# Order edges for the casts of formed right operands and for one sum of blocks, in a fused attention and expert kernel

## The chip, the cores and the metric

The program runs on one core of one Trainium2 chip. The metric is the device time of one execution in microseconds; times are medians over runs. The core's engines are TensorE (PE, with its weight loads as PEld), VectorE (DVE), ScalarE (ACT), GpSimd (POOL) and SyncE (SP), which issues nearly all DMAs here.

## The reference

Two attentions follow each other, and a weighted sum of four experts follows them. Each of 8 batches has 8 heads, 576 tokens and a head width of 64; 32 learned rows `p` are packed against `k` and `v`, and the tokens `q` then attend to those packed rows.

```python
def sm_attn(qq, kk, vv):
    s = scale * np.matmul(qq, kk.transpose(0, 1, 3, 2))
    a = np.exp(s - np.max(s, axis=-1, keepdims=True))
    return np.matmul(a / (np.sum(a, axis=-1, keepdims=True) + 1e-09), vv)
p_packed = sm_attn(p, k, v)
x = sm_attn(q, p_packed, p_packed)          # then (8 * 576, 512)
pr = domain_probs / (domain_probs.sum(-1, keepdims=True) + 1e-09)
out = sum(pr[:, e:e+1] * (np.maximum(x @ w1[e], 0) @ w2[e]) for e in range(4))
```

## The kernel before

**Units.** The 8 batches are taken in four pairs (`sb`), and the 4 experts' 1024 hidden columns in 8 chunks of 512 (`ch`). A unit is one batch and one chunk; the list `units` has 64 of them, pair by pair and chunk by chunk, the even batch ahead of the odd one (two neighbours are swapped at the start and two at the end). Below, "unit 21" is `u == 21`.

**The second product of a unit.** The product of the hidden block with `w2` is done as seven smaller products instead of eight (`ORDER`: a11, s3, s1, s2, a22, s4, a12). A left operand is either a block `a..` of the hidden activations, left by VectorE in the tile `ablk`, or a sum or difference of blocks, made by VectorE at line 598 in the tile `sblk`: s3 = a11 - a21, s1 = a21 + a22, s2 = s1 - a11, s4 = a12 - s2. Each left operand is split into a high part, which ScalarE casts (line 111, tile `st`), and a low part, which GpSimd subtracts (line 115, `st`). The order of these casts among themselves, and of the low parts among themselves, is fixed by edges from each to the one before (`marks["operand"]`). They are issued two products ahead (`LA = 2`), so the first operands of unit u + 1 are issued beside the last products of unit u.

**The right operands.** They are formed from `w2` once, while the first pair of batches is worked on (`t_form`), kept in `tt` tiles, and stored to DRAM (`td`) for later pairs. For chunk ch + 1 this is done in the odd units of the first pair from unit 3 on and in the even unit behind each: loads of b11, b12, b2, then seven steps. t1 and t3 are made ahead of step 1, t2 ahead of step 3 and t4 ahead of step 4; t1, t2 and t4 all replace the contents of b11, which step 0 casts, so t1 waits until step 0 has read it. t1 and t4 are GpSimd's, t2 and t3 VectorE's (line 639). Each step casts the high part on ScalarE (line 111, `tt<-b` or `tt<-ablk`) and subtracts the low part on GpSimd (line 115).

**Attention beside it.** `pack_unit` works on the packed rows of the next pair of batches in units 4 and 7 (first pair of batches), 17 and 20, 33 and 36, with scores at product 4 or, in units 20 and 36, at product 5. Its steps are: scores on TensorE; the maximum over keys on VectorE (line 182); the bias (184 or 186); the exponential on ScalarE (188); a transposition of the result on TensorE (line 75); a copy to SBUF (111, `at`); the product with `v`; its scaling (`ppn`, line 221 on ScalarE or 223 on VectorE); another transposition. With `relief=True`, which is the case in units 4 to 8, ScalarE first copies the scores to SBUF (line 180), and takes the bias and the scaling. `tok_unit` does the second attention in the same manner.

**First product.** `g_form` multiplies the packed rows into `w1` (tile `wraw`), ScalarE casts the result (`ghl`, 111) and VectorE leaves the low part (`ghl`, 115); `mm1_groups` multiplies it with the tokens `xh`, `xl`, and VectorE evicts the block at line 370. VectorE adds the products of the second matmul up at line 718.

**Who sets the order.** The kernel is built with a planner that works through the program in a simulated time and writes one list for each engine. On the chip each engine goes through its list in order, and semaphores stop it where data is not there. `after(ins, prev)` adds an edge that only tells the planner to put `ins` behind `prev`. TensorE's work may move between calls of `together`. PSUM holds four tiles (`dbl`) in turn, so TensorE can be about three groups of matmuls ahead of VectorE's and ScalarE's reads.

Of the kernel before, what the change touches and what calls it, by code (L numbers as in the profile page):

```python
# [42 lines left out]
def attention_moe(ctx: ExitStack, tc: tile.TileContext, q, k, v, p, dp, w1, w2, out):  # L43
# [107 lines left out]
    def pack_unit(bs, g, new, relief=False):  # L151
        nfull = S // P
        r = S - nfull * P
        kts = {}
        for b in bs:
            if g == 0:
                pts[b] = small.tile([P, NPAIR, NPK], F32, name="pt")
                nc.sync.dma_start(out=pts[b], in_=p[b])
            kts[b] = new(b, [P, 2, S], "kt")
            nc.sync.dma_start(out=kts[b], in_=k[b][:, 2 * g:2 * g + 2, :])  # L160
        yield

        def load_v(b):
            vt, vr = new(b, [P, nfull, 4 * D], "vt"), new(b, [P, 4 * D], "vr")
            behind_w1(nc.sync.dma_start(
                out=vt, in_=v[b, 0:nfull * P, g * 4 * D:(g + 1) * 4 * D].rearrange("(c p) d -> p c d", p=P),
            ), b)
            behind_w1(nc.sync.dma_start(out=vr[0:r], in_=v[b, nfull * P:S, g * 4 * D:(g + 1) * 4 * D]), b)
            return [vt[:, c, :] for c in range(nfull)] + [vr]

        vt = load_v(bs[0])
        yield
        pss = scores(bs, g, lambda b, pr, hh: pts[b][hh * D:(hh + 1) * D, pr, :], kts)
        a1s, rss = {}, {}
        for b in bs:
            nb = small.tile([P, 1], F32, name="nb")
            a1s[b] = new(b, [P, S], "a1")
            a1v, raw = a1s[b].rearrange("p (c s) -> p c s", c=2), pss[b][:, :, 0:HS]
            if relief:
                nc.scalar.copy(out=a1v, in_=raw)  # L180
                raw = a1v
            nc.vector.tensor_reduce(out=nb, in_=raw, axis=AX.XY, op=ALU.max)
            if relief:
                nc.scalar.mul(nb, nb, -SCALE)
            else:
                marks["bias", b, g] = nc.vector.tensor_scalar_mul(nb, nb, -SCALE).ins
            sm = small.tile([P, 1], F32, name="sm")
            marks["first", b, g] = nc.scalar.activation(
                out=a1v, in_=raw, func=AF.Exp, scale=SCALE, bias=nb, accum_out=sm
            ).ins  # L190
            rss[b] = small.tile([P, 1], F32, name="rs")
            if relief:
                nc.scalar.activation(out=rss[b], in_=sm, func=AF.Copy, bias=1e-9)
            else:
                nc.vector.tensor_scalar_add(rss[b], sm, 1e-9)
            nc.vector.reciprocal(out=rss[b], in_=rss[b])
        yield
        prs = slice(2 * g, 2 * g + 2)
        for b in bs:
            if b != bs[0]:  # L200
                vt = load_v(b)
            at = new(b, [P, len(SC), P], "at")
            ps = dbl()
            for c in range(nfull):
                tr(out=ps[:, 0, c * P:(c + 1) * P], in_=a1s[b][:, c * P:(c + 1) * P], identity=ident)
            tr(out=ps[0:r, 1, 0:P], in_=a1s[b][:, nfull * P:S], identity=ident)
            turn = nc.vector if (b, g) == (0, 0) else nc.scalar
            hi_of(at[:, 0:nfull, :], ps[:, 0].rearrange("p (c s) -> p c s", s=P), turn)
            marks["turned", b, g] = hi_of(at[0:r, nfull, :], ps[0:r, 1, 0:P], turn).ins
            yield  # L210
            ps = dbl()
            for c, (_, n) in enumerate(SC):
                for h in range(4):
                    p0 = h // 2 * 2 * NPK + cols(b, h % 2).start
                    mm(
                        out=ps[p0:p0 + NPK, 0, 0:D], lhsT=at[0:n, c, p0:p0 + NPK],
                        rhs=vt[c][0:n, h * D:(h + 1) * D], start=c == 0, stop=c == len(SC) - 1,
                    )
            ppn = small.tile([P, D], F32, name="ppn")
            if relief:  # L220
                nc.scalar.mul(ppn, ps[:, 0, 0:D], rss[b])
            else:
                nc.vector.tensor_scalar_mul(ppn, ps[:, 0, 0:D], rss[b])
            yield
            ps = dbl()
            tr(out=ps[0:D, 0, 0:P], in_=ppn, identity=ident)
            psv = ps[0:D, 0, 0:P].rearrange("p (j n) -> p j n", j=2)
            for hh in range(2):
                hi_of(
                    ppbd[b % 4][hh * D:(hh + 1) * D, prs, cols(b, hh)], psv[:, :, cols(b, hh)],  # L230
                    nc.scalar if relief else nc.vector,
                )
            yield
# [354 lines left out]
    def s_operand(u, i):  # L588

        name = ORDER[i] if u < LAST else PLAIN[i]  # L590
        blk = lambda n: blocks[u, n]
        if name[0] == "s":
            t = hpool.tile([P, 2, HS], F32, name="sblk", bufs=3)
            x, y, op = {
                "s1": ("a21", "a22", ALU.add), "s2": ("s1", "a11", ALU.subtract),
                "s3": ("a11", "a21", ALU.subtract), "s4": ("a12", "s2", ALU.subtract),
            }[name]
            marks["sum", u, name] = nc.vector.tensor_tensor(out=t, in0=blk(x), in1=blk(y), op=op).ins  # L598
            blocks[u, name] = t
        src = blk(name)  # L600
        st = st_tile(F32R)
        parts = hi_of(both(st, 0), src, nc.scalar).ins, lo_of(both(st, 1), src, both(st, 0), nc.gpsimd).ins
        for ins, prev in zip(parts, marks.get("operand", ())):
            after(ins, prev)
        marks["operand"] = parts
        blocks[u, "op", i] = st
# [13 lines left out]
    def t_form(ch, new, eng):  # L620
# [14 lines left out]
        for i, name in enumerate(ORDER):  # L635
            n = of[name]
            for m in {"t3": ("t1", "t3"), "t2": ("t2",), "t4": ("t4",)}.get(n, ()):
                x, y, place = how[m]
                op = eng[m].tensor_tensor(out=blk[place], in0=blk[x], in1=blk[y], op=ALU.subtract).ins
                if ch == 1 and m == "t3":  # L640
                    after(op, marks["bias", 1, 1])
                blk[m] = blk[place]
            t = wpool.tile([P, 2, 2, DH], F32R, name="tt", bufs=8)
            high = hi_of(t[:, 0], blk[n], nc.scalar)
            lo_of(t[:, 1], blk[n], t[:, 0], nc.gpsimd)
            if ch == 1 and i == 0:
                after(high.ins, marks["operand"][0])
            if ch == 1 and i in (1, 3):
                after(high.ins, marks["turned", 1, i // 2])
            marks["form"] = high  # L650
            tt[ch, i] = t
            yield
# [329 lines left out]
```

## Time and profile before

| what | value |
|---|---|
| time, median of 3 runs (lowest to highest) | 1279.35 us (1279.25 to 1279.41) |
| the profiled execution: its own time, its span | 1280.87 us, 1279.1 us |
| mean granted TensorE clock | 0.997 |
| PE, PEld busy share of the span | 98%, 92% |
| DVE, ACT, POOL busy share of the span | 75%, 38%, 67% |

The span is the time from the first to the last instruction of the profiled execution; 1.77 us of that execution's own time lie around it. The median of the runs is 1.52 us below the profiled execution's time. A row of the timeline gives the start and length of one instruction, or of several alike in a row that are drawn together (x2: two), and in brackets the idle time of that engine just before it and what ended it.

### The profile page before, as it was taken

The numbers are of one execution on the slowest core, as the hardware profiler recorded it, in microseconds if no ns is written. First come the engines' busy times: TensorE is split into PE (matmuls) and PEld (weight loads), VectorE is DVE, ScalarE is ACT, GpSimd is POOL, SyncE is SP. The second block draws the span as 40 slices with busy tenths as digits, with TensorE's granted clock in tenths as the row PEclk, the third lists the DMA queues.
The fourth block names the chain that finished last, engine by engine and source line by source line (L and its number), as shares of the span: only waits on it lengthen the run. The fifth ranks groups of instructions, "written<-read, shape, count | busy, mean of one in ns | idle before, by whom it ended". The sixth has DMA issues, their size and how long they took to land.

```text
span 1279.1 us, 26863 instructions
## 1 busy us (share of the span) xinstructions
PE 1256.6 (98%) x10764; PEld 1171.7 (92%) x10764; DVE 955.1 (75%) x1299; ACT 492.4 (38%) x888; POOL 861.2 (67%) x570
## 2 busy tenths in 40 slices
PE   6999999999999999999999999999999999999998
PEld 4789988998999999999999999999999999999998
DVE  4776777899985767997786667799679567766776
ACT  3644444636334333333324423333323533332321
POOL 3878888898995555666578454576568755556575
PEclk9999999999999999999999999999999999999999
DMA  9885656534465544545455546433446443444562
GB/s 334 337 303 186 227 172 225 185 138 169 161 221 197 172 159 128 183 163 158 133 151 172 181 145 205 144 126 125 157 126 214 148 136 116 128 155 127 178 217 100
DMA packets 91707, 223.93 MB, mean 175 GB/s; under 512 B 9280, under 2 KB 32192, under 8 KB 91584
## 3 DMA queue, kind: packets, MB, share of 16 engines
q1 hardware_dynamic: 90768, 221.92, 52.4%
q8 instruction: 86, 1.41, 0.4%
q10 hardware_dynamic: 816, 0.30, 0.1%
q14 instruction: 37, 0.30, 0.1%
HBM read 183.31 MB, written 38.87 MB: 174 GB/s over the span
## 4 chain that ended last, share of the span: by engine, by line
PE 73%; POOL 11%; DVE 10%; issue 3%; ACT 2%; DMA 2%; SPq 0%; ACTq 0%; POOLq 0%; DVEq 0%
PE dbl L70 66%; POOL st L115 7%; PE dbl L80 6%; DVE sblk L598 2%; POOL acc L749 2%; DVE acc L718 2%; DVE ablk L370 1%; DVE ghl L115 1%; POOL tt L115 1%; DMA kt<-in_k 1%; PE dbl L75 1%; POOL xl L115 1%; ACT ghl L111 1%; DVE a L257 0%; DVE s L277 0%
## 5 line engine op out<-in xcount | busy, mean ns | idle before, releaser
L70 PE MATMUL dbl<-st,tt 128*128 128x288 f32 x5388 | 766.6, 296 | 4.4 <-DVE ghl L115 1.8
L70 PEld LDWEIGHTS dbl<-st,tt 128*128 128x128 f32 x5388 | 724.7, 188 | 49.1 <-issue 28.9
L115 POOL TENSOR_TENSOR st<-sblk,st 128x576 fp32r<-128x576 f32 x252 | 397.1, 1584 | 230.5 <-ACT st L111 221.8
L70 PE MATMUL dbl<-xh,ghl 128*128 128x288 f32 x2016 | 406.4, 294 | 2.1 <-DVE ghl L115 2.1
L115 POOL TENSOR_TENSOR st<-ablk,st 128x576 fp32r<-128x576 f32 x193 | 293.5, 1524 | 137.4 <-ACT st L111 131.0
L718 DVE TENSOR_TENSOR acc<-dbl,acc 128x576 f32<-128x576 f32 x385 | 287.7, 751 | 103.3 <-PE dbl L70 101.3
L70 PEld LDWEIGHTS dbl<-xh,ghl 128*128 128x128 f32 x2016 | 321.8, 188 | 2.7 <-DVE ghl L115 2.6
L70 PE MATMUL dbl<-xl,ghl 128*128 128x288 f32 x1008 | 295.8, 294 | 0.2 <-POOL xl L115 0.2
L370 DVE SCALAR_TENSOR_TENSOR ablk<-dbl,pbt 128x576 f32<-128x576 f32 x256 | 192.3, 752 | 138.7 <-PE dbl L70 137.0
L111 ACT CAST st<-sblk 128x576 fp32r<-128x576 f32 x252 | 170.3, 676 | 275.9 <-DVE sblk L598 220.4
L111 ACT CAST st<-ablk 128x576 fp32r<-128x576 f32 x193 | 130.3, 675 | 253.6 <-PE dbl L70 230.1
L70 PEld LDWEIGHTS dbl<-xl,ghl 128*128 128x128 f32 x1008 | 188.9, 188 | 0.5 <-POOL xl L115 0.5
L598 DVE TENSOR_TENSOR sblk<-ablk 128x576 f32<-128x576 f32 x126 | 134.4, 1067 | 9.6 <-DVE ablk L370 0.5
L111 ACT CAST ghl<-dbl 128x512 fp32r<-128x512 f32 x128 | 72.7, 588 | 114.1 <-DVE ghl L115 58.4
L115 DVE TENSOR_TENSOR ghl<-dbl,ghl 128x512 fp32r<-128x512 f32 x124 | 83.3, 687 | 20.5 <-ACT ghl L111 18.5
L598 DVE TENSOR_TENSOR sblk<-ablk,sblk 128x576 f32<-128x576 f32 x63 | 78.3, 1242 | 5.3
L80 PE MATMUL dbl<-wraw,ppbd 64*32 64x512 f32 x1024 | 68.2, 597 | 0.0
L115 POOL TENSOR_TENSOR tt<-b,tt 128x512 fp32r<-128x512 f32 x42 | 62.8, 1505 | 2.1 <-ACT tt L111 2.0
L598 DVE TENSOR_TENSOR sblk<-sblk,ablk 128x576 f32<-128x576 f32 x63 | 57.7, 916 | 1.3
L749 POOL TENSOR_TENSOR acc<-acc,acc 128x576 f32<-128x576 f32 x28 | 43.5, 1563 | 12.6 <-DVE acc L718 12.5
L716 ACT COPY acc<-dbl 128x576 f32<-128x576 f32 x56 | 35.9, 641 | 36.3 <-PE dbl L70 36.3
L80 PEld LDWEIGHTS dbl<-wraw,ppbd 64*32 64x32 f32 x1024 | 15.2, 105 | 20.9 <-issue 18.7
(117 smaller groups left out, 464.8 us busy)
## 6 DMA issues: line engine op xcount, KB each, us to landing
tt<-td SPq DMA_DIRECT2D x192, 512.0 KB, 4.3
wraw<-in_w SPq DMA_DIRECT2D x136, 256.0 KB, 3.6
td<-tt SPq DMA_DIRECT2D x56, 512.0 KB, 4.1
pbt<-pnd SPq DMA_DIRECT2D x32, 288.0 KB, 4.2
out<-acc SPq DMA_DIRECT2D x31, 288.0 KB, 2.4
kt<-in_k SPq DMA_DIRECT2D x14, 576.0 KB, 5.9
kt<-in_q SPq DMA_DIRECT2D x14, 576.0 KB, 6.1
vt<-in_v SPq DMA_DIRECT2D x15, 512.0 KB, 4.9
```

Of the source, the lines that this page charges most:

```text
L70: res = nc.tensor.matmul(**kw)
L75: on_pe(nc.tensor.transpose(**kw))
L80: ins = nc.tensor.matmul(**kw).ins
L111: return nc.scalar.copy(out=dst, in_=src)
L115: return eng.tensor_tensor(out=dst, in0=src, in1=hi.bitcast(F32), op=ALU.subtract)
L370: res = nc.vector.scalar_tensor_tensor(out=a, in0=ps[:, :, 0:HS], scalar=0.0, in1=pbt[b][:, c * HS:(c + 1) * HS].rearrange("p (o t) -> p o ...
L598: marks["sum", u, name] = nc.vector.tensor_tensor(out=t, in0=blk(x), in1=blk(y), op=op).ins
L716: nc.scalar.copy(out=accs[b, i], in_=psv)
L718: nc.vector.tensor_tensor(out=accs[b, i], in0=psv, in1=accs[b, i], op=ALU.add)
L749: eng.tensor_tensor(out=m[dst], in0=m[x], in1=m[y], op=op)
```

## The change

Three order edges are added, and two marks that they need. No instruction is added or taken away.

- The first sum that is issued behind a `pack_unit` (from unit 4 on) is put behind that unit's first maximum on VectorE. By the order of issue this is the s3 of the following unit: of units 5, 8, 18, 21, 34 and 37 (and that of unit 4, behind a maximum that is long done by then).
- In chunks 2 to 7 each cast of a formed right operand is put behind the newest cast of a left operand. Before, only step 0 of chunk 1 had this edge.
- The same casts are put behind ScalarE's newest attention step that has been issued: the first exponential of the newest `pack_unit`, or the newest scaling `ppn` (with relief).

```diff
+            largest = nc.vector.tensor_reduce(out=nb, in_=raw, axis=AX.XY, op=ALU.max).ins
+            if b == bs[0]:
+                marks["largest"] = largest
...
+            marks["attention"] = [marks["first", bs[0], g]]
...
             if relief:
-                nc.scalar.mul(ppn, ps[:, 0, 0:D], rss[b])
+                marks["attention"] = [nc.scalar.mul(ppn, ps[:, 0, 0:D], rss[b]).ins]
...
             marks["sum", u, name] = nc.vector.tensor_tensor(out=t, in0=blk(x), in1=blk(y), op=op).ins
+            if u > 3 and "largest" in marks:
+                after(marks["sum", u, name], marks.pop("largest"))
...
             high = hi_of(t[:, 0], blk[n], nc.scalar)
             lo_of(t[:, 1], blk[n], t[:, 0], nc.gpsimd)
-            if ch == 1 and i == 0:
+            if ch > 1 or ch == 1 and i == 0:
                 after(high.ins, marks["operand"][0])
+            if ch > 1:
+                for prev in marks.get("attention", ()):
+                    after(high.ins, prev)
```

## Rows read from the trace of the kernel before

**Rows 1.** The page: busy time, share of the span and instructions of each engine.

```profile
PE 1256.6 (98%) x10764; PEld 1171.7 (92%) x10764; DVE 955.1 (75%) x1299; ACT 492.4 (38%) x888; POOL 861.2 (67%) x570
```

**Rows 2.** Waits of TensorE, 60 to 1260 us: total, times, longest.

```profile
PE dbl L70 <- DVE ghl L115: 3.9, 6, 1.8
PE dbl L75 <- ACT a L188: 1.1, 2, 0.8
PE dbl L75 <- ACT ppn L221: 1.1, 2, 0.7
```

**Rows 3.** Timeline of TensorE at its stalls, 166 to 782 us.

```profile
169.06 0.30 PE L75 MATMUL dbl<-ident,ppn 128*64 128x128 f32 x1 [0.67 <-ACT ppn L221]
...
207.17 0.76 PE L75 MATMUL dbl<-ident,a 128*128 128x128 f32 x5 [0.83 <-ACT a L188]
...
274.71 2.47 PE L70 MATMUL dbl<-st,tt 128*128 128x288 f32 x17 [0.62 <-DVE acc L718]
...
308.53 3.42 PE L70 MATMUL dbl<-st,tt 128*128 128x288 f32 x24
...
314.62 0.40 PE L70 MATMUL dbl<-xh,ghl 128*128 128x288 f32 x1 [1.75 <-DVE ghl L115]
...
315.46 4.82 PE L70 MATMUL dbl<-st,tt 128*128 128x288 f32 x24
...
776.84 0.77 PE L75 MATMUL dbl<-ident,a 128*128 128x128 f32 x5 [0.28 <-ACT a L188]
```

**Rows 4.** Windows: busy time of each engine, granted clock, DMA.

```profile
245.00:273.00 28.00, 28.00 (x228) 26.00 (x227) 27.34 (x33) 15.44 (x40) 27.77 (x18) 1.00 0.47 159
...
316.00:318.00 2.00, 2.00 (x10) 2.00 (x10) 2.00 (x4) 1.67 (x3) 2.00 (x2) 0.50 0.04 8
```

**Rows 5.** Timeline of ScalarE, 168 to 169 us.

```profile
168.18 0.62 ACT L111 CAST tt<-b 128x512 fp32r<-128x512 f32 x1 [2.46 <-DMA b<-in_w]
168.70 0.31 ACT L221 ACTIVATE ppn<-dbl,rs 128x64 f32<-128x64 f32 x1
```

**Rows 6.** Timeline of ScalarE, 205 to 207 us.

```profile
205.64 0.61 ACT L111 CAST tt<-b 128x512 fp32r<-128x512 f32 x1
...
206.26 0.76 ACT L188 ACTIVATE a<-a,nb 128x576 f32<-128x576 f32 x1
```

**Rows 7.** Timeline of VectorE, 202 to 206 us.

```profile
202.53 1.73 DVE L598 TENSOR_TENSOR sblk<-sblk,ablk 128x576 f32<-128x576 f32 x1
204.19 1.40 DVE L182 TENSOR_REDUCE nb<-a 128x1 f32<-128x576 f32 x2
```

**Rows 8.** Timeline of VectorE, 456 to 467 us.

```profile
456.76 0.76 DVE L598 TENSOR_TENSOR sblk<-ablk 128x576 f32<-128x576 f32 x1
...
464.17 0.74 DVE L598 TENSOR_TENSOR sblk<-sblk,ablk 128x576 f32<-128x576 f32 x1
464.84 1.41 DVE L182 TENSOR_REDUCE nb<-dbl 128x1 f32<-128x576 f32 x2
```

**Rows 9.** Timelines of GpSimd and of TensorE, 455 to 476 us.

```profile
461.53 1.44 POOL L115 TENSOR_TENSOR st<-sblk,st 128x576 fp32r<-128x576 f32 x1 [5.00 <-ACT st L111]
...
470.40 1.85 PE L70 MATMUL dbl<-st,tt 128*128 128x288 f32 x12
```

**Rows 10.** Timelines of GpSimd and of VectorE, 245 to 274 us.

```profile
246.82 3.60 POOL L115 TENSOR_TENSOR tt<-b,tt 128x512 fp32r<-128x512 f32 x2
...
273.20 0.69 DVE L639 TENSOR_TENSOR ablk<-b,ablk 128x512 f32<-128x512 f32 x1 [0.58 <-POOL b L639]
```

**Rows 11.** Timelines of VectorE and of GpSimd, 303 to 315 us.

```profile
303.15 0.76 DVE L283 TENSOR_TENSOR a<-a,s 128x576 f32<-128x576 f32 x1
...
312.14 1.83 DVE L283 TENSOR_TENSOR a<-a,s 128x576 f32<-128x576 f32 x1
313.89 0.68 DVE L115 TENSOR_TENSOR ghl<-dbl,ghl 128x512 fp32r<-128x512 f32 x1
...
311.56 1.79 POOL L639 TENSOR_TENSOR b<-ablk,b 128x512 f32<-128x512 f32 x1
```

More of the change, by code (lines that the diff above doesn't have):

```diff
@@ L181, in pack_unit @@
                 raw = a1v
-            nc.vector.tensor_reduce(out=nb, in_=raw, axis=AX.XY, op=ALU.max)
+            largest = nc.vector.tensor_reduce(out=nb, in_=raw, axis=AX.XY, op=ALU.max).ins
+            if b == bs[0]:
+                marks["largest"] = largest
             if relief:
```

## The prediction, made before the changed kernel was seen

> **What bounds the kernel now.** I read the page first: TensorE is busy for 1256.6 of 1279.1 us, and every other engine has room [rows 1]. A kernel like this gets shorter only where TensorE stands still, or where its clock is low. So the second view was who makes TensorE wait, with the start-up and the tail cut off by a window from 60 to 1260 us. The reader is to see how little there is: 3.9 us for the low part of `ghl`, 1.1 us for the exponential of line 188 and 1.1 us for the scaling `ppn` [rows 2]; what I do not show there adds 1.3 us. That is the whole stock from which an edit of the order can earn, with one addition: after one of these stalls the clock fell.
>
> The third view was the timeline of TensorE at these stalls, and then ScalarE and VectorE at the same times, to see what stood ahead of the late instruction in its list. Four stalls matter. At 169.06 the turning of `ppn` came 0.67 us late, at 207.17 that of an attention block 0.83 us late, at 776.84 another 0.28 us late, and at 314.62 a matmul of the first product 1.75 us late [rows 3]. Behind the last one the granted clock was 0.50 from 316 to 318 us [rows 4], that is the level of 1.2 GHz. The two bursts of 24 equal matmuls on either side of it show the price: 4.82 us behind the stall and 3.42 us ahead of it, so 1.40 us [rows 3]. Behind the stall of 0.83 us the clock did not fall. The rest of `ghl`'s 3.9 us is spread over five short waits that no part of this change touches.
>
> **What each part does.** All three edits are order edges between instructions of one engine. They cost no instruction, no semaphore and no transfer; what they can cost is that something starts later.
>
> *The casts behind the newest attention step.* At 168.18 ScalarE runs a cast of a right operand, step 0 of chunk 4, which is issued only with unit 7. The planner had pulled it forward, and it waited 2.46 us for its load; `ppn`, at 168.70, stood behind it [rows 5]. This is the cause of TensorE's 0.67 us. With the edge that cast stands behind `ppn`; the product with `v` ends ahead of it, so `ppn` can run while TensorE is still in the product that it does before the turning. I take the whole 0.67 us.
>
> *The same edge at unit 7.* The exponential starts at 206.26, right behind a cast of a right operand of 0.61 us at 205.64 [rows 6]. Its maximum is late as well: the two maxima start at 204.19, behind a sum that took 1.73 us [rows 7]. With the casts gone from there, the first bias can be taken when the first maximum ends, which is half of 1.40 us behind 204.19, at 204.89; the exponential then ends near 205.9 with its 0.76 us and one short bias step ahead of it, instead of 207.0. That is 1.1 us, more than the stall of 0.83 us, which I take as gone whether or not the maximum moves.
>
> *The sum behind the first maximum.* Unit 21 stands for the four places of the later pairs. The sum that gets the edge is s3, the one at 456.76, some 8 us ahead of the two maxima at 464.84; the sum right ahead of them, at 464.17, is s2 and has no edge [rows 8]. So this edit does not take away what stands directly ahead of the maximum. It empties VectorE's list and GpSimd's earlier (the low part of s3 is the one at 461.53 [rows 9]), and lets the planner put the maximum ahead of s2. If that happens the maximum comes 0.74 us earlier, and the stall of 0.28 us at 776.84, in the twin of this place in unit 37, goes. I take these 0.28 us; at unit 21 itself TensorE's row shows no wait worth a bracket. In units 18 and 34 nothing stalled.
>
> The price of moving s3: its low part is needed when product 1 of unit 21 starts at 470.40 [rows 9]. Behind the first maximum (464.84 and half of 1.41) s3 takes 0.76 us, to 466.31 [rows 8]. Its cast takes about 0.70 us (0.62 us [rows 5] for 512 columns, and this one has 576), and the low part 1.44 us [rows 9], which ends at 468.45: 1.9 us to spare. I take nothing, and keep the other end for a rival. In units 8 and 18 the scores come one product earlier, and there is more to spare.
>
> The Trainium skill (SBUF — State Buffer, the section on two separate sides) says that VectorE with two SBUF inputs and GpSimd share a pair of ports as an exclusive lock, so that the one that starts second waits for the whole instruction of the other. By that rule a sum that is moved into a stretch where GpSimd works could take a whole low part longer. The rows agree where GpSimd is busy (1.83 us against 0.76 us for the same multiplication [rows 11]); at unit 21 the low part that GpSimd would be doing is that of s3 itself, so the sum above does not change.
>
> *The casts behind the newest left operand.* In the even units of the first pair two or three casts of right operands stood ahead of left operands. Their low parts on GpSimd (such as the two at 246.82, 3.60 us [rows 10]) now come behind those of the left operands, which are needed first, while the right ones have about two products until their use. No wait of TensorE on `st` above 0.5 us exists that this could take away, so I put it at nothing. What hides the later casts is that distance; if it is used up, the price is the second rival's.
>
> The sum: 0.67 + 0.83 + 0.28 = 1.78 us. The profiled execution's 1280.87 us become 1279.09 us; the runs' median lies 1.52 us below the profiled time, so 1277.57, say **1277.6 us**. Its own range: 1278.6 if only the 0.67 us are earned (or as much is lost elsewhere), and 1276.7 if 0.43 us, what is left of the waits for `ppn` (1.1 less 0.67 [rows 2]), and half a microsecond of short waits go too.
>
> **The rivals.** A change of 0.2% (2.6 us) is about what a measurement of this kernel can tell from none, so the sum itself is just inside.
>
> *The long stall goes too.* The stall at 314.62 ends when VectorE has left the low part of `ghl` at 313.89. Ahead of it stood a multiplication of 1.83 us, which overlapped GpSimd's t1 at 311.56; the same multiplication took 0.76 us at 303.15 [rows 11]. With the edge, t1 of chunk 7 must come later than before: its step 0 can no longer be done one unit early. If t1 leaves the multiplication alone, the stall shrinks by 1.07 us to 0.68, less than the 0.83 us behind which the clock stayed up, and the 1.40 us of low clock go as well: 1277.6 - 1.07 - 1.40 = **1275.1 us**. Against it: another low part of GpSimd may take t1's place.
>
> *GpSimd falls behind and makes it slower.* From 245 to 273 us GpSimd is busy for 27.77 of 28 us [rows 4]. At its end VectorE, in t3 of chunk 6 at 273.20, waits 0.58 us for GpSimd's t1 [rows 10], the eviction behind it is late, and TensorE waits 0.62 us [rows 3]. If the two low parts at 246.82 (3.60 us) must wait for their casts and GpSimd finds nothing to do, t1 moves by up to 3.60 us; step 0 of chunk 6, which must precede t1, moves into the same stretch. From there each microsecond is paid one for one by VectorE's list and TensorE, and past 1.75 us of stall [rows 3] the clock falls for another 1.40 us: 1277.6 + 3.60 + 1.40 = **1282.6 us**. It decides (slower by 0.2%) from about 2.9 us of delay on. Against it: t4 and left operands can fill the hole, the planner sees the delay and can put t3 further back, and casts of right operands have slack.
>
> The Trainium skill's page TensorE: Matmul & The Clock Gate (the section on the HAM clock gate) says that the clock is gated by how busy the engine has been and is half when it was idle; the one fall here, behind the 1.75 us, agrees, and no row here shows one behind a shorter wait.
>
> *The gain is eaten by late left operands.* If the planner puts s3 behind both maxima (466.25 [rows 8]) and one more sum of up to 1.73 us [rows 7], and ScalarE does one exponential of 0.76 us [rows 6] ahead of its cast, the low part ends at 466.25 + 1.73 + 0.76 + 0.76 + 0.70 + 1.44 = 471.64, 1.2 us late. In units 21 and 37 together that is 2.4 us: 1277.6 + 2.4 = **1280.0 us**, no change. For it speaks that s3 is issued behind both maxima; against it, that GpSimd stood idle for 5.00 us ahead of this low part [rows 9], so nothing is queued there.
>
> *The edge on the sum does nothing,* since s2 and not s3 stands ahead of the maximum: then 0.28 us less, 1277.9 us, within the forecast's own range.
>
> **How the numbers follow.** I give the forecast 0.42, the shorter long stall 0.18, the eaten gain 0.22 and GpSimd's delay 0.18. Faster by over 0.2% means below 1276.8: the second case nearly whole and something under half of the forecast's, whose range runs to 1276.7 and whose other small waits I do not know: 0.36. Slower means above 1281.9: most of the last case, 0.18. The rest, 0.46, is within 0.2%. The range runs from 1274.8, just below the long stall's case, to 1282.0, which leaves out the worst of GpSimd's delay.
>
> **What would show it.** Right: on ScalarE, no cast `tt` between a product with `v` and its `ppn` near 168 us, and none among bias and exponential near 206; TensorE's waits for lines 188 and 221 under 0.5 us together, where they were 2.2. In units 21 and 37, s3 behind the maximum, and its low part ends ahead of product 1. Waits of ScalarE's `tt` casts for loads of b gone. Wrong: a new bracket of over 0.5 us on TensorE in units 9 to 14 with VectorE at line 639 waiting for GpSimd; product 1 of unit 21 or 37 waiting for GpSimd's `st`; or a second stretch of clock 0.50. The prediction as a whole is wrong if the stall at 314.62 is gone or doubled, since it alone with its clock is larger than all that I count.

## The result, and the profile after

The changed kernel takes 1288.03 us (median of 6 runs, 1287.71 to 1288.93), the kernel before beside it 1279.46 us. The ratio over all runs is 1.0056, with a 95% interval from 1.0039 to 1.0073: slower by 0.56%, where 1277.6 us and a range from 1274.8 to 1282.0 us were forecast. (The two medians alone stand at 1.0067; one run of before took 1285.75 us.) The profiled execution took 1288.25 us with a span of 1286.5 us, 7.4 us more than the span of 1279.1 us before; the medians differ by 8.6 us, because the profiled execution of before lay 1.4 us above its median and that of the changed kernel 0.2 us.

The page shows the same work on each engine and a longer span. This is its first part, beside [rows 1]:

```profile
PE 1259.5 (98%) x10764; PEld 1173.2 (91%) x10764; DVE 957.7 (74%) x1299; ACT 492.1 (38%) x888; POOL 862.2 (67%) x570
```

So the question is again who makes TensorE stand. The view of its waits, from 60 to 1270 us, beside [rows 2] (lines have moved by 2 to 8: 190 is the exponential, 224 `ppn`, 726 the adding up, 601 the sums, 644 the differences t, 373 the eviction):

```profile
PE dbl L70 <- DVE ghl L115: 6.4, 7, 2.5
PE dbl L75 <- ACT a L190: 2.1, 2, 1.1
PE dbl L70 <- DVE acc L726: 2.1, 2, 1.1
PE dbl L70 <- POOL st L115: 1.7, 3, 0.9
PE dbl L75 <- ACT ppn L224: 0.4, 1, 0.4
```

The waits for `ppn` fell from 1.1 to 0.4 us. Those for `ghl`, for the exponential, for the adding up and for GpSimd's left low parts grew. The timeline of TensorE says where, beside [rows 3]:

```profile
168.29 0.37 PE L70 MATMUL dbl<-st,tt 128*128 128x288 f32 x1 [1.09 <-DVE acc L726]
...
194.18 0.37 PE L70 MATMUL dbl<-st,tt 128*128 128x288 f32 x1 [1.00 <-DVE acc L726]
...
262.26 0.40 PE L70 MATMUL dbl<-st,tt 128*128 128x288 f32 x1 [0.90 <-POOL st L115]
...
280.46 0.37 PE L70 MATMUL dbl<-st,tt 128*128 128x288 f32 x1 [2.50 <-DVE ghl L115]
...
319.44 0.40 PE L70 MATMUL dbl<-xh,ghl 128*128 128x288 f32 x1 [1.82 <-DVE ghl L115]
...
473.73 0.44 PE L75 MATMUL dbl<-ident,a 128*128 128x128 f32 x2 [1.06 <-ACT a L190]
...
784.26 0.33 PE L75 MATMUL dbl<-ident,a 128*128 128x128 f32 x1 [1.06 <-ACT a L190]
```

The two stalls ahead of transpositions at 169 and 207 us are gone. New are those where unit 6 begins (168.29) and in units 7, 10 and 11, where unit 11 had one of 0.62 us; the one in unit 13 (319.44) is nearly as it was; in unit 37 0.28 us have become 1.06, and unit 21, which had none, waits 1.06 us too.

To compare kernels I take the time between the starts of two products, which leaves the start-up out (it differs by up to 5 us between executions, without regard to the change). "4.4" is product 4 of unit 4. Each entry is worked out from the starts of the matmuls in one trace, in us; a star marks a stretch in which the granted clock was 0.50 for some 3.4 us.

| kernel | 4.4 to 6.2 | 7.0 to 7.4 | 7.4 to 8.3 | 10.0 to 12.0 | 12.0 to 20.0 | 20.0 to 22.0 | 36.0 to 38.0 |
|---|---|---|---|---|---|---|---|
| before | 36.89 | 9.58 | 18.20 | 38.03 | 158.80* | 41.67 | 41.82 |
| after | 37.49 | 10.81 | 17.36 | 41.02 | 160.13* | 42.60 | 42.60 |
| e1 sum only | 37.49 | 9.58 | 19.32 | 37.97 | 158.83 | 42.59 | 42.60 |
| e2 operand edge only | 36.01 | 9.58 | 19.33 | 38.15 | 160.45 | 41.66 | 41.67 |
| e3 attention edge only | 36.00 | 9.58 | 17.16 | 41.02 | 159.48 | 41.66 | 41.66 |
| e4 step 0 free | 36.76 | 9.58 | 17.35 | 38.14 | 160.47* | 42.59 | 42.59 |
| e5 no sum edge | 36.00 | 9.58 | 17.77 | 42.50* | 159.29* | 41.66 | 41.79 |
| e6 sum behind the bias | 36.00 | 9.58 | 17.83 | 42.52* | 158.55 | 41.32 | 41.32 |
| e7 t1 first | 36.63 | 9.58 | 17.35 | 38.86 | 160.93 | 42.60 | 42.60 |
| e8 step 0 free, no sum edge | 36.00 | 9.58 | 17.16 | 38.14 | 160.36* | 41.65 | 41.79 |
| e9 attention edge in 4 chunks | 36.00 | 9.58 | 17.16 | 41.01 | 159.68 | 41.32 | 41.32 |
| e10 both edges in 4 chunks | 36.00 | 9.58 | 17.77 | 40.99 | 159.79* | 41.32 | 41.32 |
| e11 the change in 4 chunks | 37.49 | 10.81 | 17.36 | 41.01 | 159.63 | 42.59 | 42.60 |
| e12 attention edge in 3 chunks | 36.00 | 9.58 | 17.16 | 37.99 | 158.82 | 41.32 | 41.32 |

From product 2.0 to the end the changed kernel takes 7.15 us more, of which the columns hold 7.02: 0.60 + 1.23 - 0.84 + 2.99 + 1.33 + 0.93 + 0.78. Three mechanisms are behind most of it; the 1.33 us of 12.0 to 20.0 stay unexplained.

**Units 9 to 11: GpSimd runs dry and then comes late.** The timelines of ScalarE, GpSimd and VectorE after:

```profile
231.33 0.31 ACT L224 ACTIVATE ppn<-dbl,rs 128x64 f32<-128x64 f32 x1 [0.18 <-PE dbl L70]
231.55 0.61 ACT L111 CAST tt<-b 128x512 fp32r<-128x512 f32 x1
...
240.60 3.93 ACT L270 ACTIVATE a<-a,m 128x32 f32<-128x32 f32 x18
244.44 0.66 ACT L111 CAST st<-ablk 128x576 fp32r<-128x576 f32 x1
245.00 0.62 ACT L111 CAST tt<-b 128x512 fp32r<-128x512 f32 x1
...
245.18 1.44 POOL L115 TENSOR_TENSOR st<-ablk,st 128x576 fp32r<-128x576 f32 x1 [3.17 <-ACT st L111]
...
249.74 1.81 POOL L644 TENSOR_TENSOR b<-b,b 128x512 f32<-128x512 f32 x1
...
276.51 1.30 POOL L644 TENSOR_TENSOR b<-ablk,b 128x512 f32<-128x512 f32 x1
277.75 1.41 POOL L115 TENSOR_TENSOR st<-ablk,st 128x576 fp32r<-128x576 f32 x1
...
277.85 1.87 DVE L644 TENSOR_TENSOR ablk<-b,ablk 128x512 f32<-128x512 f32 x1 [2.57 <-POOL b L644]
```

Read it from the top. The cast of a right operand at 231.55 is step 0 of chunk 5, and the new edge puts it behind `ppn` at 231.33, the newest attention step. Everything that formed chunk 5 then came one step later, until the cast of operand 10.0 (244.44) and the next cast of a right operand (245.00) fell behind a run of 18 exponentials of the second attention, 3.93 us at 240.60. GpSimd had nothing to do for 3.17 us ahead of 245.18. t4, at 249.74, had been at 243.37 us in the kernel before, and of these 6.4 us the kernel was only 1.2 us behind when unit 9 began. From here GpSimd's list is nearly full (17.72 us busy of the 19 from 262 to 281), so what it lost it does not make good: in unit 11, t1 comes at 276.51, VectorE stands in t3 for 2.57 us (0.58 before, [rows 10]), and then t3 itself takes 1.87 us instead of 0.69, because GpSimd began its next low part 0.10 us ahead of it. TensorE waits 2.50 us, where it had waited 0.62 us for the adding up [rows 3]. In unit 10 it waits 0.90 us for a late left low part of GpSimd. Units 10 and 11 take 1.10 and 1.89 us longer, which is the 2.99 us of the table.

**Units 21 and 37: the sums stand between maximum and bias.** VectorE and ScalarE in unit 21, after:

```profile
469.40 1.42 DVE L182 TENSOR_REDUCE nb<-dbl 128x1 f32<-128x576 f32 x2 [0.43 <-PE dbl L80]
470.75 1.42 DVE L601 TENSOR_TENSOR sblk<-ablk 128x576 f32<-128x576 f32 x2
472.08 0.20 DVE L188 TENSOR_SCALAR nb<-nb 128x1 f32<-128x1 f32 x2
...
471.60 1.34 ACT L111 CAST st<-sblk 128x576 fp32r<-128x576 f32 x2 [5.21 <-DVE sblk L601]
472.85 0.74 ACT L190 ACTIVATE a<-dbl,nb 128x576 f32<-128x576 f32 x1
```

s3 now waits for the maximum, as the edge says, and s1, which does not need the edge, follows it. Both stand ahead of the two short bias steps; their two casts stand ahead of the exponential. The exponential starts 2.0 us behind the second maximum (which ends at 470.82), and TensorE waits 1.06 us for it. Of the 2.0 us, 1.5 pass until the bias steps are done at 472.28; the last 0.6 us are the second cast, as the exponential starts only when it ends (1.34 us behind 471.60).

**Unit 5: the same edge holds back a sum that had been ready.** VectorE after, and below it VectorE in e5, which has no edge on the sum:

```profile
141.04 0.76 DVE L182 TENSOR_REDUCE nb<-a 128x1 f32<-128x576 f32 x1 [1.10 <-ACT a L180]
141.72 1.42 DVE L601 TENSOR_TENSOR sblk<-ablk 128x576 f32<-128x576 f32 x2
```

```profile
134.14 1.64 DVE L601 TENSOR_TENSOR sblk<-ablk 128x576 f32<-128x576 f32 x1
...
140.47 1.41 DVE L182 TENSOR_REDUCE nb<-a 128x1 f32<-128x576 f32 x2
```

Without the edge s3 of unit 5 runs in a quiet place at 134.14; with it, at 141.72, among maxima, sums and the adding up. That is 7.58 us, or 6.0 without the start-up, which was 1.56 us longer after. Later in the unit t3, at 156.18, and t2, at 161.91, take 1.90 us each beside GpSimd's low parts, and TensorE pays 1.09 us at 168.29. That the edge on the sum costs time here is shown by e1 and e5 below; the path from s3 to these two differences is read from the rows, and no run takes it apart.

The promised gains are there as well: ScalarE runs `ppn` at 168.17 with no cast of a right operand ahead of it, and the exponential of unit 7 at 205.24, 1.02 us earlier than in [rows 6] although the kernel is 2.0 us behind at product 7.4.

```profile
168.17 0.31 ACT L224 ACTIVATE ppn<-dbl,rs 128x64 f32<-128x64 f32 x1
...
205.24 0.78 ACT L190 ACTIVATE a<-a,nb 128x576 f32<-128x576 f32 x1
```

### The profile page after: what moved, and what is told of

Same layout as the page of the kernel before. It is cut to its first block, busy times and chain, and to the rows that moved or that the text cites. A ratio compares the mean times of both kernels' runs of the same rounds, so it can differ in the third digit from the quotient of the medians.

```text
span 1286.5 us, 26876 instructions
## 1 busy us (share of the span) xinstructions
PE 1259.5 (98%) x10764; PEld 1173.2 (91%) x10764; DVE 957.7 (74%) x1299; ACT 492.1 (38%) x888; POOL 862.2 (67%) x570
## 4 chain that ended last, share of the span: by engine, by line
PE 72%; POOL 13%; DVE 9%; issue 3%; ACT 2%; DMA 1%; SPq 0%; ACTq 0%; POOLq 0%; DVEq 0%
PE dbl L70 65%; POOL st L115 8%; PE dbl L80 6%; POOL acc L757 2%; DVE sblk L601 2%; POOL tt L115 2%; DVE acc L726 1%; DVE ghl L115 1%; DVE ablk L373 1%; POOL xl L115 1%; PE dbl L75 1%; ACT ghl L111 1%; DVE a L260 0%; ACT st L111 0%; DVE m L265 0%
## 5 line engine op out<-in xcount | busy, mean ns | idle before, releaser
L115 POOL TENSOR_TENSOR st<-sblk,st 128x576 fp32r<-128x576 f32 x252 | 402.2, 1606 | 231.8 <-ACT st L111 229.7
L601 DVE TENSOR_TENSOR sblk<-ablk 128x576 f32<-128x576 f32 x126 | 130.3, 1039 | 8.1
L757 DVE TENSOR_TENSOR acc<-acc,acc 128x576 f32<-128x576 f32 x28 | 34.1, 1223 | 0.6
```

Source lines behind the costliest of these rows:

```text
L115: return eng.tensor_tensor(out=dst, in0=src, in1=hi.bitcast(F32), op=ALU.subtract)
L757: eng.tensor_tensor(out=m[dst], in0=m[x], in1=m[y], op=op)
```

## The experiments

Diffs are against the changed kernel. Medians are given with the ratio to the kernel before on the same chip.

**e1: the sum's edge alone.**

```diff
-            if ch > 1 or ch == 1 and i == 0:
+            if ch == 1 and i == 0:
                 after(high.ins, marks["operand"][0])
-            if ch > 1:
-                for prev in marks.get("attention", ()):
-                    after(high.ins, prev)
```

> Only the edge from the first maximum to the sum is left. Theory 1 (the time is lost because step 0 of each later chunk is held back, so GpSimd's t1 is late and VectorE stands in t3) expects none of TensorE's new waits near 167, 193, 262 and 278 us here, and only the waits for the exponential in units 21 and 37 longer by 0.9 us each: about +1.9 us less up to 0.8 us at unit 8, so 1280 to 1281.5 us. Theory 2 (the sum edge is the main loss, by way of a fuller VectorE list from unit 5 on) expects 1283 us or more, with new waits between 150 and 300 us.

1284.58 us, ratio 1.0034 (1.0021 to 1.0047). Units 21 and 37 wait 1.06 us each, as after; products 4.4 to 6.2 take 37.49 us, as after; 7.4 to 8.3 take 1.1 us more than before. So the edge on the sum loses time by itself, in three kinds of places. Units 10 to 12 are as before. Theory 1 had the losses of units 21 and 37 right and, with them, the time too low; the new waits of up to 0.90 us from 161 to 208 us are those of theory 2.

**e2: the casts' edge behind the newest left operand alone.**

```diff
-            if u > 3 and "largest" in marks:
-                after(marks["sum", u, name], marks.pop("largest"))
...
-            if ch > 1:
-                for prev in marks.get("attention", ()):
-                    after(high.ins, prev)
```

> Only the edge from the newest left cast to the casts of right operands is left; it holds step 0 of every chunk back into its own unit, though less far than the edge on attention. Theory 1 expects VectorE to wait in t3 for t1 as in the changed kernel, with a TensorE wait of 2 us or more in unit 11 and one near 1 us in unit 7, and 1281.5 to 1284 us; the 0.67 us at ppn near 168 us gone. Theory 2 expects about the time before, 1278.5 to 1280 us.

1281.84 us, ratio 1.0007 (0.9994 to 1.0020). Products 4.4 to 6.2 gain 0.9 us, 7.4 to 8.3 lose 1.1 (a wait of 1.73 us at 205.74), 12.0 to 20.0 lose 1.6. Units 10 to 12 take 0.1 us more than before: this edge alone does not make GpSimd late there, and the waits that theory 1 expected in units 7 and 11 did not come.

**e3: the casts' edge behind the newest attention step alone.**

```diff
-            if u > 3 and "largest" in marks:
-                after(marks["sum", u, name], marks.pop("largest"))
...
-            if ch > 1 or ch == 1 and i == 0:
+            if ch == 1 and i == 0:
                 after(high.ins, marks["operand"][0])
```

> Only the edge from the newest attention step to the casts of right operands is left; it holds back step 0 of chunks 3, 4 and 5, while those of chunks 6 and 7 come after the last attention step anyway and stay early. Theory 1 expects the long wait in unit 11 (2.5 us in the changed kernel) to be back at 0.6 us, the waits at 168 and 206 us gone, and 1278 to 1280 us. A rival, that any new order in this stretch brings VectorE and GpSimd into each other's way, expects new waits of over 1 us and 1281 us or more.

1280.87 us, ratio 1.0007 (0.9991 to 1.0023). Both gains are here, 0.9 us in 4.4 to 6.2 and 1.0 us in 7.4 to 8.3, and so is the whole loss of units 10 to 12, 3.0 us (waits of 2.13 us at 263.53 and 1.26 us at 280.49). One edge gives the one and takes the other. Theory 1, which expected no long wait in unit 11, fell; the rival's waits of over 1 us came, though here the longer one is in unit 10, where TensorE waits for GpSimd's left low part.

**e4: the whole change, but step 0 of chunks 2 to 7 without its edges.**

```diff
-            if ch > 1 or ch == 1 and i == 0:
+            if ch > 1 and i > 0 or ch == 1 and i == 0:
                 after(high.ins, marks["operand"][0])
-            if ch > 1:
+            if ch > 1 and i > 0:
```

> The changed kernel with step 0 of chunks 2 to 7 freed of both new edges; steps 1 to 6 keep them, and so does the sum. Theory 1 expects t1 early again, the waits in units 7 and 11 down to what they were before (none, and 0.6 us), and the time between before and the change: 1279.5 to 1281.5 us, with the loss in units 21 and 37 left. Theory 2 and the rival expect little or no gain on the changed kernel: 1285 us or more.

1283.45 us, ratio 1.0024 (1.0015 to 1.0034): 4.6 us less than the changed kernel. The waits of units 7, 10 and 11 are gone, 1.23 and 2.88 us by the table; units 21 and 37 keep their 1.06. So the first cast of a chunk is the one whose delay costs in units 7, 10 and 11. The time stays 2 us above theory 1's range: 12.0 to 20.0 take 1.7 us more than before.

**e5: the whole change without the edge on the sum.**

```diff
-            if u > 3 and "largest" in marks:
-                after(marks["sum", u, name], marks.pop("largest"))
```

> The change with both edges on the casts and without the edge on the sum of blocks. If the three edges act each by itself (theory), TensorE's waits of 1.06 us in units 21 and 37 go (products 20.0 to 22.0 take 41.7 us again instead of 42.6, and 36.0 to 38.0 41.7 instead of 42.6), the waits of 1.0 us in unit 7 and 2.5 us in unit 11 stay, and the time is 1288.0 - 1.7 = 1286.3 us. Rival: the edges act together, because the sum alone cost 5 us where its two places account for 1.7; then the waits of units 7 and 11 become smaller too, and the time is 1282 to 1284 us.

1284.39 us, ratio 1.0019 (1.0009 to 1.0029). Both the theory and its rival are half right. Units 21 and 37 come back (41.66 and 41.79 us) and unit 11 keeps its wait (2.48 us, with a fall of the clock behind it that the changed kernel did not have); but unit 7's 1.23 us and unit 5's loss, 1.5 us against the changed kernel, go as well. Unit 7's loss needs both kinds of edges, as neither e1 nor e5 has it. In unit 5 the sum's edge alone gives the 37.49 us (e1), and what the casts' edges earn there alone (36.00 us) doesn't come beside it. How little it takes shows unit 7, where t3 does the same work in both kernels. GpSimd and VectorE after, and below them in e5:

```profile
191.39 1.42 POOL L115 TENSOR_TENSOR st<-ablk,st 128x576 fp32r<-128x576 f32 x1
...
191.46 1.91 DVE L644 TENSOR_TENSOR ablk<-b,ablk 128x512 f32<-128x512 f32 x1 [1.76 <-POOL b L644]
```

```profile
188.91 1.44 POOL L115 TENSOR_TENSOR st<-ablk,st 128x576 fp32r<-128x576 f32 x1 [0.72 <-ACT st L111]
...
188.23 0.69 DVE L642 TENSOR_TENSOR ablk<-b,ablk 128x512 f32<-128x512 f32 x1 [0.59 <-POOL b L642]
```

After, GpSimd's low part starts 0.07 us ahead of t3 and t3 takes 1.91 us; in e5 t3 starts first and takes 0.69. The difference, 1.22 us, is about the 1.23 us of the table. The Trainium skill (SBUF — State Buffer, the section on who interferes with whom) says that VectorE with two inputs in SBUF contends with a GpSimd instruction that reads SBUF, and that the order in which the two are issued decides which one blocks; the two pairs of rows agree.

**e6: the sum behind the second bias instead of the first maximum.**

```diff
-            if b == bs[0]:
-                marks["largest"] = largest
...
                 marks["bias", b, g] = nc.vector.tensor_scalar_mul(nb, nb, -SCALE).ins
+                marks["largest"] = marks["bias", b, g]
```

> The whole change, but the sum comes behind the bias of the second batch (the small multiplication behind the second maximum) instead of behind the first maximum. Theory: what costs 0.93 and 0.78 us in units 21 and 37 is that s3 and s1, 0.67 us each, stand between the second maximum and the bias, and the exponentials wait for the bias; so both stretches come back to 41.7 us, and the time is 1286.3 us with the waits of units 7 and 11 as they were. Rival: the left operands' casts that stand ahead of the exponential on ScalarE hold it back anyway; then TensorE still waits 0.6 us or more there, and s3, which is later still, adds to it: 1288 us or more.

1282.78 us, ratio 1.0013 (1.0000 to 1.0027). With relief no mark is set, so units 5 and 8 are free of the edge. Units 21 and 37 take 41.32 us, 1.28 us less than after and 0.35 and 0.50 less than before. VectorE and ScalarE in unit 21:

```profile
468.23 1.42 DVE L182 TENSOR_REDUCE nb<-dbl 128x1 f32<-128x576 f32 x2 [0.43 <-PE dbl L80]
469.57 0.27 DVE L186 TENSOR_SCALAR nb<-nb 128x1 f32<-128x1 f32 x2
469.76 0.75 DVE L600 TENSOR_TENSOR sblk<-ablk 128x576 f32<-128x576 f32 x1
...
469.81 0.75 ACT L189 ACTIVATE a<-dbl,nb 128x576 f32<-128x576 f32 x1 [4.59 <-DVE nb L186]
```

The exponential now starts 0.2 us behind the second maximum, where it started 2.0 us behind, and s3, which is no earlier, costs nothing. So the loss in these units was not s3's own delay but what s3 and s1 held up. The theory named the bias and the rival the casts ahead of the exponential; e6 moves both out of the way and doesn't separate them, and by the rows of the changed kernel each had a part, some 1.3 and 0.6 us. The time is 3.5 us below the theory's, as units 5 and 7 are free of their losses as well.

**e7: t1 one step earlier.**

```diff
         for i, name in enumerate(ORDER):
             n = of[name]
-            for m in {"t3": ("t1", "t3"), "t2": ("t2",), "t4": ("t4",)}.get(n, ()):
+            first = {"b11": ("t1",), "t3": ("t3",)} if ch > 1 else {"t3": ("t1", "t3")}
+            for m in {**first, "t2": ("t2",), "t4": ("t4",)}.get(n, ()):
```

> The whole change, but in chunks 2 to 7 GpSimd's difference t1 is issued ahead of the low part of step 0 (one step earlier) and no longer behind it. Theory: t1 stood behind the low part that the held-back cast released late, and VectorE waited for it in t3 with its evictions queued behind; so t3 no longer waits 1.8 us in unit 7 and 2.6 us in unit 11, products 7.0 to 7.4 take 9.6 us instead of 10.8 and 11.0 to 12.0 18.4 instead of 20.2, and the time is 1288.0 - 3.0 = 1285 us. Rival: GpSimd as a whole is behind there (its left low parts in unit 10 and 11 are late by themselves), and t1 is only the last of a queue; then the waits move to the left low parts and the time stays at 1287 to 1289 us.

In this kernel step 0 of chunks 2 to 7 casts the tile b11 after t1 has replaced its contents, so one right operand of seven holds other values; the instructions are the same, but step 0's cast now waits for t1. 1283.44 us, ratio 1.0029 (1.0013 to 1.0045), 4.6 us less than the changed kernel; unit 7 is at 9.58 us, and 10.0 to 12.0 take 38.86. GpSimd, VectorE and TensorE in unit 11:

```profile
269.06 1.80 POOL L645 TENSOR_TENSOR b<-ablk,b 128x512 f32<-128x512 f32 x1
...
270.90 0.69 DVE L645 TENSOR_TENSOR ablk<-b,ablk 128x512 f32<-128x512 f32 x1 [0.58 <-POOL b L645]
...
272.40 0.37 PE L70 MATMUL dbl<-st,tt 128*128 128x288 f32 x1 [1.10 <-DVE acc L727]
```

t3 again waits 0.58 us and takes 0.69, and TensorE waits 1.10 us instead of 2.50. The loss in unit 10 went too, which the theory had not said; in 12.0 to 20.0, 0.8 us more than after came in. ScalarE in units 9 and 10 shows that the cure is not in unit 11 alone:

```profile
227.00 0.31 ACT L224 ACTIVATE ppn<-dbl,rs 128x64 f32<-128x64 f32 x1 [0.18 <-PE dbl L70]
227.21 0.61 ACT L111 CAST tt<-b 128x512 fp32r<-128x512 f32 x1
...
237.60 0.62 ACT L111 CAST tt<-b 128x512 fp32r<-128x512 f32 x1
238.12 3.93 ACT L270 ACTIVATE a<-a,m 128x32 f32<-128x32 f32 x18
```

Step 0 of chunk 5 still stands right behind `ppn`, as in the changed kernel, but t1 no longer waits for it, and the later cast (237.60) is ahead of the 18 exponentials again. So what the late step 0 of chunk 5 hands on, it hands on through t1.

**e8: the edges on the casts, steps 1 to 6 only, and none on the sum.** The diffs of e4 and e5 together.

> Only the two edges on the casts, and these on steps 1 to 6 of chunks 2 to 7; step 0 is free and the sum has no edge. Theory: both losses gone, the two gains kept (products 4.4 to 6.2 at 36.0 to 36.8 us instead of 36.9, 7.4 to 8.3 at 17.2 to 17.4 instead of 18.2, none of the waits of 0.67 and 0.83 us); the rest as with step 0 free: 1283.45 - 1.7 = 1281.7 us or, if units 12 to 18 come out as before, 1278.5 us, 1 us less than before. Rival (any new order of these casts brings VectorE and GpSimd in each other's way somewhere in units 10 to 18): 1280.5 to 1283 us, with new waits of 0.5 to 1.4 us in units 11 to 13.

1280.69 us, ratio 0.9997 (0.9983 to 1.0012): no difference from before that shows. Both losses are gone and both gains are there, but 12.0 to 20.0 take 1.6 us more than before and 8.3 to 9.0 take 0.8 us more (a wait of 0.59 us at 222.31). The rival was right about that.

**e9, e10, e11: the edges in chunks 2 to 5 alone.** e9 has the attention edge alone and e10 both edges, each with e6's sum; e11 is the change itself with both edges cut to these chunks. e10's diff, behind e6's:

```diff
-            if ch > 1 or ch == 1 and i == 0:
+            if 1 < ch < 6 or ch == 1 and i == 0:
                 after(high.ins, marks["operand"][0])
-            if ch > 1:
+            if 1 < ch < 6:
                 for prev in marks.get("attention", ()):
```

> Only the edge of the casts behind the newest attention step, and only in chunks 2 to 5; the sum comes behind the second bias; no edge behind the left operands. Theory: the attention edge gives its two gains (products 4.4 to 6.2 in 36.0 instead of 36.9 us, 7.4 to 8.3 in 17.2 instead of 18.2), the loss of units 10 to 12 belongs to chunk 6 alone and stays away (10.0 to 12.0 in 38.0 us), and the sum behind the bias gives 0.35 and 0.5 us in units 20 to 22 and 36 to 38: 2.8 us less than the kernel before in the same state of the clock, so 1276.5 to 1278 us. Rival: the loss of 1.4 us that every variant so far showed in units 12 to 16 comes in from the new order upstream: 1278 to 1280 us.

> Both edges on the casts, in chunks 2 to 5 alone, and the sum behind the second bias. Theory: products 4.4 to 6.2 in 36.0 us, 7.4 to 8.3 in 17.8, 10.0 to 12.0 in 38.0 as before the change, 20 to 22 and 36 to 38 in 41.3: 2.2 us less than the kernel before in the same state of the clock, 1277 to 1278.6 us. Rival, as for the run beside it: a new loss of some 1.4 us in units 12 to 16, 1278.6 to 1280 us.

> The whole change, but its edges on the casts stand in chunks 2 to 5 alone. Theory (the losses are local): the waits of units 10 and 11 (0.90 and 2.50 us) go with chunk 6's edges, 3.0 us; the stretches before do not depend on it, so products 4.4 to 6.2 stay at 37.5 and 7.0 to 7.4 at 10.8, and units 21 and 37 keep their 1.06: 1285 us, in the same state of the clock. Rival (the losses hang together): units 5 to 8 change too, or the wait of unit 11 stays at over 1.5 us because GpSimd comes late from unit 7: 1287 us or more.

1281.51 us (ratio 1.0008, 0.9991 to 1.0025), 1282.19 us (1.0021, 1.0009 to 1.0033) and 1286.43 us (1.0048, 1.0033 to 1.0063). My theory fell in all three: I had put the late t1 of unit 11 down to chunk 6, whose t1 it is. Without any edge on chunk 6, 10.0 to 12.0 still take 41.0 us in each. The delay is made earlier and arrives there. That sent me back to units 9 and 10, to the chain shown above: it begins with the cast of step 0 of chunk 5.

**e12: the attention edge in chunks 2 to 4 alone, the sum behind the bias.** As e9, with one number changed:

```diff
-            if 1 < ch < 6:
+            if 1 < ch < 5:
                 for prev in marks.get("attention", ()):
```

> The casts' edge behind the newest attention step in chunks 2 to 4 alone, no edge behind the left operands, the sum behind the second bias. Theory now: it is chunk 5's casts, held back in units 9 and 10, that let GpSimd idle at 241 to 245 us and leave it too much afterwards; without their edge products 10.0 to 12.0 take 38.0 us again, the gains of the earlier chunks (36.0 us for 4.4 to 6.2, 17.2 for 7.4 to 8.3) and of the sum behind the bias (41.3 us twice) stay, 2.8 us in all: 1276.5 to 1278 us. Rival: GpSimd is so full there that any new order upstream, even one that is early, gives 10.0 to 14.0 a new wait of 1 us or more: 1278 to 1281 us.

1278.29 us against 1280.98, ratio 0.9985 (0.9966 to 1.0003); the shortest execution is 1276.80 us, that of before 1279.21. The interval still holds 1, so faster is likely and not proved, and the median lies 0.3 us above the theory's range. From e9 only chunk 5's edge differs, and 10.0 to 12.0 fall from 41.01 to 37.99 us: the theory's number. e4 freed step 0 of all chunks and e12 all steps of chunk 5; no run frees step 0 of chunk 5 alone, but the two meet there. ScalarE and GpSimd in units 9 and 10 of e12:

```profile
236.00 0.62 ACT L111 CAST tt<-b 128x512 fp32r<-128x512 f32 x1
...
236.80 0.68 ACT L111 CAST st<-ablk 128x576 fp32r<-128x576 f32 x1
237.39 3.94 ACT L269 ACTIVATE a<-a,m 128x32 f32<-128x32 f32 x18
...
238.63 1.44 POOL L115 TENSOR_TENSOR st<-ablk,st 128x576 fp32r<-128x576 f32 x1
```

Here both casts run ahead of the 18 exponentials, and GpSimd has work while they run. A window of 4 us that starts 0.4 us behind the first of the 18 shows it in one number, at 241.00 after and at 237.80 in e12. The columns are the busy times of PE, PEld, DVE, ACT and POOL, the granted clock, the DMA share and GB/s; after, then e12:

```profile
241.00:245.00 4.00, 4.00 (x33) 4.00 (x32) 4.00 (x5) 4.00 (x18) 1.01 (x1) 1.00 0.98 305
```

```profile
237.80:241.80 4.00, 4.00 (x32) 4.00 (x31) 3.83 (x6) 4.00 (x19) 4.00 (x3) 1.00 0.89 333
```

GpSimd is busy for 1.01 of 4 us after and for all 4 in e12. The traces of all 14 kernels agree: in the seven in which the two casts stand behind the 18 exponentials (after, e3, e5, e6, e9, e10, e11) GpSimd is idle there for 3.14 to 3.17 us and 10.0 to 12.0 take 40.99 to 42.52 us; in the other seven it is idle for 0.57 us at most at a time, and they take 37.97 to 38.86 us.

## Why the prediction was wrong, step by step

**What held.** TensorE's waits are what the time is made of. The attention edge does earn the two terms for it: the 0.67 us at `ppn` and the 0.83 us in units 7 and 8 are gone, and e3, which has this edge alone, shows 0.89 us in 4.4 to 6.2 and 1.04 us in 7.4 to 8.3 against the 1.50 us predicted. (The first is not this edge's alone: e2 earns 0.88 us there with the other edge on the casts.) The maximum did come ahead of s2 in unit 21, as hoped (s2 is at 472.87), and e6 shows that this is worth 0.35 and 0.50 us once nothing stands between maximum and exponential. The long stall in unit 13 stayed (1.82 us), so the 1.07 and 1.40 us of the rival that wanted it gone did not come. The 1.40 us were not there to be had, as the last section shows.

**The steps that failed.** Two costs were taken as nothing.

The first is the casts: the sum took no charge for their being later, and gave the mechanism to the rival *GpSimd falls behind*. That mechanism came about, at 2.99 us in place of the rival's 3.60, without the fall of the clock: 1.89 us in unit 11 in the view that I had named, VectorE in t3 behind GpSimd's t1 with TensorE waiting, and 1.10 us in unit 10, where TensorE waits for a left low part, which I had not named. Where it begins I had wrong. I looked to the operand edge and to the low parts at 246.82; e2 has that edge and no loss there. It is the attention edge on the first cast of chunk 5, 49 us earlier than the stall, and between lies a step that I had not looked at: ScalarE's 18 exponentials in a row, behind which the casts fall once they are a little late. My words "casts of right operands have slack" were true for their use by TensorE and not for GpSimd, which lives on them.

The second is the sum, where I wrote "I take nothing". I worked out when s3's low part would be ready and found 1.9 us to spare; that was right, and e6 shows a still later s3 at no cost. What I didn't work out is whom a sum in the new place holds up: s1 follows it, and the two stand ahead of the bias, their casts ahead of the exponential, and the transposition waits. The price is 0.93 and 0.78 us in units 21 and 37, in place of a gain of 0.28. And I weighed units 8 and 18 and not unit 5, where the edge moved s3 by 6.0 us into a crowd. "It empties VectorE's list and GpSimd's earlier" left out that the work comes back between the maximum and the bias.

**The sum.** The 7.02 us of the table: 2.99 for chunk 5's casts, 1.71 for bias and exponential held up in units 21 and 37, 0.60 in 4.4 to 6.2 (the sum's edge, which loses as much alone in e1; the 0.89 that the casts' edges earn alone is lost beside it), 1.23 in unit 7 where both kinds act together, -0.84 earned in 7.4 to 8.3, and 1.33 in 12.0 to 20.0 that no experiment ties to one edge (in the variants, between -0.25 and +2.13 us came in there). The range failed because each rival stood by itself: with one loss on each side of the change, both came, 2.99 + 1.71, and their total with the crowding lies beyond the worst that I had priced singly. One slip of the sum's own range changes nothing: without the 0.83 and the 0.28 us it is 1278.7 and not 1278.6 us.

## What to carry to other kernels

For an order edge ask not only whether the moved instruction is still in time, but who stands behind its new place on its engine, and whether what it feeds runs dry. An engine with over 99% of a stretch busy ([rows 4]) pays for an idle moment some 30 us earlier; look for the long run on the feeding engine that a late instruction falls behind. When a loss shows at one chunk's instructions, take the edge from the chunk before as well: here the symptom was chunk 6's and the cause chunk 5's.

## What the runs showed of the hardware

Whether the clock falls behind a stall doesn't follow from the stall's length alone. Behind the stall in unit 13 the granted clock went to 0.50, the level of 1.2 GHz, at 1.70 us (e10), 1.75 (before), 1.82 (after, e5), 1.92 (e8) and 1.93 us (e4), and stayed at 1.00 at 1.67 (e11), 1.71 (e9), 1.70 (e3), 1.73 (e1), 1.74 (e12), 1.81 (e2) and 1.82 us (e6, e7). The 2.50 us in unit 11 brought no fall after, the 2.48 and 2.46 us in the same place of e5 and e6 did. The windows behind the stall in unit 13, after and in e12:

```profile
320.50:323.50 3.00, 3.00 (x14) 3.00 (x14) 3.00 (x5) 0.99 (x3) 3.00 (x3) 0.50 0.02 5
```

```profile
313.00:316.00 3.00, 2.89 (x23) 2.69 (x22) 2.92 (x6) 2.04 (x5) 3.00 (x3) 1.00 0.00 0
```

The Trainium skill (TensorE: Matmul & The Clock Gate, on the HAM clock gate) says that the clock follows how busy the engine has been; these rows agree in that each of these falls comes behind a stall, and show that stalls of one length in one place may or may not bring one. A fall costs less than its own stretch: with it unit 13 takes 1.2 us longer (21.08 us before, 19.84 to 19.91 in e9, e11 and e12), but units 14 and 15 then take 37.2 us instead of 38.0, and at unit 20 nothing is left of it: 12.0 to 20.0 take 158.80 us before, with the fall, and 158.83 and 158.82 in e1 and e12, without. So the 1.40 us that the prediction read from two bursts of matmuls were not a price that the whole kernel paid. Presumably the other engines, which had been nearly the bound, catch up in the meantime; no run takes that apart.

The second is how sharp the collision of VectorE and GpSimd is: 0.07 to 0.10 us of order decide between 0.7 and 1.9 us for the same kind of difference. The slow ones stand above, behind a low part that had begun 0.07 and 0.10 us earlier. In the kernel before, t2 of unit 5 begins 0.07 us ahead of a low part, and it is GpSimd that takes longer, 1.90 us instead of 1.44:

```profile
154.78 0.68 DVE L639 TENSOR_TENSOR b<-b,b 128x512 f32<-128x512 f32 x1
...
154.85 1.90 POOL L115 TENSOR_TENSOR st<-ablk,st 128x576 fp32r<-128x576 f32 x1
```

A small change upstream moves such starts. That may be why e9 and e10, which have no edge on a cast behind chunk 5, lost 0.9 and 1.0 us in 12.0 to 20.0, and e12 nothing; no run shows it.
